# Grouped-query attention over a cached K and V: units of four kv heads of two sequences, K turned by VectorE in 32x32 blocks instead of by TensorE

## The chip, the cores and the metric

One core of one Trainium2 chip runs the whole program. The metric is the time of one execution of the program on the device in microseconds (us); the median of several executions counts. TensorE (PE) multiplies matrices, VectorE (DVE) and ScalarE (ACT) work on elements, GpSimd (POOL) does small copies, SyncE (SP) issues the transfers from the memory of the device (HBM) to the memory of the core, which has 128 partitions.

## The reference

Eight sequences bring 4 new tokens each. Queries are projected from x, scored against a cached K of 2048 keys, and the softmax weighs a cached V. 32 query heads share 8 kv heads, four to one. All inputs are bf16.

```python
# B, Sq, D = 8, 4, 512;  Hq, Hkv, Sk, Dh = 32, 8, 2048, 128
q = (x @ wq).reshape(B, Sq, Hq, Dh).transpose(0, 2, 1, 3)
k = jnp.repeat(k_cache, 4, axis=1)          # k_cache, v_cache: [8, 8, 2048, 128]
v = jnp.repeat(v_cache, 4, axis=1)
scores = jnp.einsum("bhqd,bhkd->bhqk", q, k) * (Dh ** -0.5)
p = softmax(scores, axis=-1)
o = jnp.einsum("bhqk,bhkd->bhqd", p, v)
return o.transpose(0, 2, 1, 3).reshape(B, Sq, Hq * Dh) @ wo   # [8, 4, 512]
```

K and V are 33.6 MB each, wq and wo 4.2 MB each: 75.5 MB are read once.

## The kernel before

A unit is two kv heads of one sequence; there are 32 units. Its K is one transfer of 1 MiB (`load_k`, L113): partition g*64+s holds 32 consecutive keys of head g, a row of 8 KiB in HBM. V is loaded in the same way (`load_v`, L123). K has 7 buffers and V has 6. All loads are issued by SP in one written order. At most eight transfers are under way at once, because each issue waits for the completion of the transfer eight before it.

Scores need K with the head dimension on the partitions. `transpose_part` (L193) does a quarter of a unit: PE turns four 128x128 tiles, each element a pair of bf16 taken as one 32-bit word, into PSUM (L198), and VectorE copies the quarter to the core's memory (L200). `scores` (L254) multiplies it with block-diagonal queries, four products beside each other in four 32-column groups of the array (L261), and ScalarE takes the exponential and its sum (L272). `probs_to_keys` (L277) turns the probabilities on PE and ScalarE copies them into a block-diagonal tile (L286). `values` (L316) holds a 128x128 piece of V as weights and streams 32 columns of probabilities through it, 32 times a unit. `norms` and `finish` divide by the sums. `to_tokens`, `to_wo_rows` and `project` bring the result to the rows in which wo is loaded and multiply with wo. Half of wo is loaded late, into the place of wq.

The order of each engine's work is the order in which the program is written (`manual_schedule`). The main loop (L405) runs iteration n with K of unit n turned, scores of n-1 and values of n-2. Each engine takes its instructions in this order, and waits on semaphores for the others.

Of the kernel before, what the change touches and what calls it, by code (L numbers as in the profile page):

```python
# [8 lines left out]
BF16 = mybir.dt.bfloat16  # L9
FP32 = mybir.dt.float32  # L10
EXP = mybir.ActivationFunctionType.Exp


@with_exitstack
def kernel(
# [18 lines left out]
    G2 = Hkv // 2  # L34
    C = 2 * Sk // 128
    NQ = 2 * rep * Sq
    HQ = rep * Sq
    J = C // 2
    JT = J // 4
    HP = 2 * rep  # L40
    scale = float(Dh) ** -0.5
    NU = G2 * B
    KB = 7
    VB = 6
    A = 2
    KA = A + 1
    WR = HP
    DH = D // 2


    NE, WE, WM, WN = 40, 8, 5, 64
    assert NE * WE + 128 * WM + WN == HP * 128
    AX = mybir.AxisListType.X
    ADD = mybir.AluOpType.add
    assert Dh == 128 and C == 32 and NQ == 32 and G2 == 4

    const = ctx.enter_context(tc.tile_pool(name="const", bufs=1))
    wpool = ctx.enter_context(tc.tile_pool(name="wpool", bufs=1))
    kpool = ctx.enter_context(tc.tile_pool(name="kpool", bufs=KB))
    vpool = ctx.enter_context(tc.tile_pool(name="vpool", bufs=VB))  # L60
    ktpool = ctx.enter_context(tc.tile_pool(name="ktpool", bufs=6))
    small = ctx.enter_context(tc.tile_pool(name="small", bufs=2))
    psum_k = ctx.enter_context(tc.tile_pool(name="psum_k", bufs=3, space=bass.MemoryType.PSUM))
    psum_s = ctx.enter_context(tc.tile_pool(name="psum_s", bufs=1, space=bass.MemoryType.PSUM))
    psum_t = ctx.enter_context(tc.tile_pool(name="psum_t", bufs=1, space=bass.MemoryType.PSUM))
    psum_o = ctx.enter_context(tc.tile_pool(name="psum_o", bufs=1, space=bass.MemoryType.PSUM))
    psum_e = ctx.enter_context(tc.tile_pool(name="psum_e", bufs=1, space=bass.MemoryType.PSUM))
    psum_l = ctx.enter_context(tc.tile_pool(name="psum_l", bufs=1, space=bass.MemoryType.PSUM))


    order = ctx.enter_context(tc.manual_schedule())


    pad0 = const.tile([128, 192], BF16, name="pad0")
    wo_e = const.tile([64, WE, D], BF16, name="wo_e")
    wo_n = const.tile([WN, D], BF16, name="wo_n")
    wo_m = const.tile([128, WM, D], BF16, name="wo_m")
    x_sb = const.tile([T, D], BF16, name="x_sb")
    wq_sb = wpool.tile([128, R, HqDh], BF16, tag="w", name="wq_sb")
    xT_sb = const.tile([128, R, T], BF16, name="xT_sb")  # L80
    qT_all = const.tile([128, G2, B, HP, Sq], BF16, name="qT_all")


    q_bd = const.tile([128, G2, 2, B, 2, 2, HQ], BF16, name="q_bd")
    pick = const.tile([128, 2, 2, Dh // 2], BF16, name="pick")
    ident4 = const.tile([128, 128], FP32, name="ident4")

    groups = [(0,), (1, 2), (3,)]
    oT = [const.tile([128, HP, len(ps), B, Sq], BF16, name=f"oT{ps[0]}") for ps in groups]
    out_sb = const.tile([2 * T, DH], BF16, name="out_sb")  # L90
    oP12 = const.tile([128, WR, 2, T], BF16, name="oP12")
    nat_sb = const.tile([2 * T, HP * 128 + 24 * WE], BF16, name="nat_sb")
    oP3 = const.tile([128, WR, T], BF16, name="oP3")
    oP = [None, oP12[:, :, 0, :], oP12[:, :, 1, :], oP3[:, :, :]]
    oE = const.tile([64, WE, T], BF16, name="oE")
    oM = const.tile([128, WM, T], BF16, name="oM")
    oN = const.tile([WN, T], BF16, name="oN")
    ident = const.tile([128, 128], BF16, name="ident")
    by_q = const.tile([128, HQ], FP32, name="by_q")
    ones = const.tile([128, 128], FP32, name="ones")  # L100
    pad = const.tile([128, 96], BF16, name="pad")
    probs = [const.tile([128, C, 2, HQ], BF16, name=f"probs{i}") for i in range(3)]

    units = [(p, b) for p in range(G2) for b in range(B)]
    ks = [None] * NU
    vs = [None] * NU

    def load_k(u):
        if u >= NU:
            return  # L110
        p, b = units[u]
        ks[u] = kpool.tile([128, C, Dh], BF16, tag="k_sb", name="k_sb")
        nc.sync.dma_start(  # L113
            ks[u][:, :, :],
            k_cache[b, 2 * p : 2 * p + 2].rearrange("g (s c) d -> (g s) c d", c=C),
        )

    def load_v(u):
        if u >= NU:
            return  # L120
        p, b = units[u]
        vs[u] = vpool.tile([128, C, Dh], BF16, tag="v_sb", name="v_sb")
        nc.sync.dma_start(  # L123
            vs[u][:, :, :],
            v_cache[b, 2 * p : 2 * p + 2].rearrange("g (s c) d -> (g s) c d", c=C),
        )

    def load_wo_e(i):

        hi, m = divmod(i, 4)  # L130
        rows = wo[: NE * WE, :].rearrange("(q r) j -> q r j", r=WE)
        a, b = hi * 32 + m, hi * NE // 2 + m
        nc.sync.dma_start(wo_e[a : a + 17 : 4, :, :], rows[b : b + 17 : 4, :, :])

    def load_wo_m():
        nc.sync.dma_start(wo_n[:, :], wo[HP * 128 - WN : HP * 128, :])
        nc.sync.dma_start(
            wo_m[:, :, :], wo[NE * WE : HP * 128 - WN, :].rearrange("(q r) j -> q r j", r=WM)
        )

    def load_wo(p, r0, n):
        rows = wo[p * HP * 128 : (p + 1) * HP * 128, :].rearrange("(q r) j -> q r j", r=WR)
        nc.sync.dma_start(wo_sb[:, p - 1, r0 : r0 + n, :], rows[:, r0 : r0 + n, :])

    load_k(0)
    nc.sync.dma_start(wq_sb[:, :, :], wq.rearrange("(p r) n -> p r n", r=R))
    nc.sync.dma_start(x_sb[:, :], x.flatten_outer_dims())
    loads = []
    for u in range(NU + KA):
        if 1 <= u <= 8:  # L150
            loads.append(("e", u - 1))
        if 0 < u < NU:
            loads.append(("k", u))
        if u == NU + 2:
            loads.append(("m", 0))
        if u >= KA - 1 and u - KA + 1 < NU:
            loads.append(("v", u - KA + 1))
    loads.reverse()

    def load_ready(nk, nv):  # L160

        while loads:
            kind, u = loads[-1]
            if kind in "em":
                loads.pop()
                load_wo_e(u) if kind == "e" else load_wo_m()
                continue
            if u >= (nk + KB if kind == "k" else nv + VB):
                return
            loads.pop()  # L170
            (load_k if kind == "k" else load_v)(u)

    nc.gpsimd.memset(wo_e[:, :, :], 0.0)
    load_ready(0, 0)

    make_identity(nc, ident[:])
    make_identity(nc, ident4[:])
    for e in range(2):
        for g in range(2):
            nc.vector.tensor_copy(  # L180
                out=pick[:, e, g, :], in_=ident[:, :].rearrange("d (k e) -> d e k", e=2)[:, e, :]
            )
    nc.vector.memset(q_bd[:, :, :, :, :, :, :], 0.0)
    for t in probs:
        nc.vector.memset(t[:, :, :, :], 0.0)
    nc.vector.memset(ones[:, :], 1.0)
    nc.vector.tensor_reduce(
        out=by_q[:, :], in_=ident4[:, :].rearrange("p (c q) -> p q c", q=HQ), axis=AX, op=ADD
    )
# [296 lines left out]
```

## Time and profile before

| What | Value |
|---|---|
| median of three runs | 190.75 us (190.39 to 193.14) |
| span of the profiled execution, first to last instruction | 187.5 us (its own whole time is not listed) |
| median less span | 3.25 us |
| busy: PE, VectorE, ScalarE, GpSimd | 143.8, 108.6, 69.5, 4.6 us |
| bytes moved, mean rate | 75.92 MB, 405 GB/s |
| rate of DMA from 20 to 165 us | 424 to 425 GB/s |
| mean granted clock of TensorE | 0.954 |

Busy time is time in which an engine executes; the span also has its waits. A matmul that is pipelined with others has a duration longer than the step from one to the next, so PE's costs are read from steps where there are rows of them. A group's row gives the line, the engine, the operation, output and inputs, the shapes, the count, the busy time, the mean duration, and the idle time before with what ended it.

### The profile page before, as it was taken

Reading aid. Unit: us, or ns where it says so; the run is one execution under the profiler, and the core shown is the slowest. Engines: PE = TensorE matmul, PEld = TensorE weight load, DVE = VectorE, ACT = ScalarE, POOL = GpSimd, SP = SyncE. Lnnn points to the kernel's source line nnn. Section 1 sums busy time; section 2 is a strip of 40 time slices with the busy share of each in tenths; the row PEclk is TensorE's granted clock in tenths of the full one; section 3 lists DMA queues with packets and bytes.
Section 4 is the critical chain, followed back from the end, with each engine's and each line's share of the span. In section 5 each row is a group of like instructions: output and inputs, shape, how many; then the busy total and the mean of one; then the engine's idle time right before and its main releaser. Section 6 shows DMA issues by size and latency. Waiting matters only on the chain.

```text
span 187.5 us, 5636 instructions
## 1 busy us (share of the span) xinstructions
PE 143.8 (77%) x2474; PEld 119.1 (63%) x2474; DVE 108.6 (58%) x217; ACT 69.5 (37%) x202; POOL 4.6 (2%) x9
## 2 busy tenths in 40 slices
PE   0516799977879988898788888787787888878493
PEld 0506488866658867786676766566676677667272
DVE  0850698757527766577565657575565666663120
ACT  2001664553324444153344444433344443425200
POOL 8100000000000000000000000000000000000000
PEclk9975999999969999999999999999999999999759
DMA  5999999999999999999999999999999999999970
GB/s 204 467 447 379 421 435 416 425 426 425 425 425 428 421 423 423 430 421 428 425 428 421 428 425 418 428 428 418 430 426 419 425 426 428 419 426 408 409 277 12
DMA packets 10984, 75.92 MB, mean 405 GB/s; under 512 B 1288, under 2 KB 1448, under 8 KB 2600
## 3 DMA queue, kind: packets, MB, share of 16 engines
q1 hardware_dynamic: 10912, 75.55, 96.2%
q8 instruction: 19, 0.31, 0.6%
q14 instruction: 5, 0.04, 0.1%
q10 hardware_dynamic: 48, 0.02, 0.0%
HBM read 75.53 MB, written 0.03 MB: 403 GB/s over the span
## 4 chain that ended last, share of the span: by engine, by line
DMA 92%; PE 6%; SPq 0%; issue 0%; ACT 0%; DVE 0%
DMA k_sb<-in_k_cache_dram 58%; DMA v_sb<-in_v_cache_dram 18%; DMA wo_m<-in_wo_dram 9%; DMA wq_sb<-in_wq_dram 8%; PE out_ps L397 3%; PE kp L198 1%; PE o_ps L321 1%; PE nat L345 0%; SPq L113 0%; PE perm L367 0%; PE s_ps L261 0%; ACT out_sb L453 0%; DVE oT L332 0%
## 5 line engine op out<-in xcount | busy, mean ns | idle before, releaser
L200 DVE COPY kt<-kp 128x1024 bf16<-128x1024 bf16 x128 | 82.3, 685 | 38.6 <-PE kp L198 38.4
L198 PE MATMUL kp<-ident,k_sb 128*128 128x128 f32 x512 | 71.3, 284 | 24.3 <-DMA k_sb<-in_k_cache_dram 22.7
L198 PEld LDWEIGHTS kp<-ident,k_sb 128*128 128x128 f32 x512 | 57.0, 144 | 36.0 <-issue 18.5
L286 ACT COPY probs<-pt 64x512 bf16<-64x512 bf16 x64 | 37.1, 580 | 53.1 <-PE pt L280 52.7
L272 ACT ACTIVATE s_sb<-s_ps 128x256 bf16<-128x256 f32 x64 | 24.0, 380 | 34.1 <-PE s_ps L261 21.7
L321 PE MATMUL o_ps<-probs,v_sb 128*128 128x32 bf16 x1024 | 30.7, 177 | 2.0 <-DMA v_sb<-in_v_cache_dram 1.2
L321 PEld LDWEIGHTS <-v_sb 128*128 128x128 bf16 x1024 | 29.8, 96 | 3.7 <-DMA v_sb<-in_v_cache_dram 2.8
L261 PE MATMUL s_ps<-kt,q_bd 128*32 128x256 bf16 x512 | 20.9, 282 | 0.0
L261 PEld LDWEIGHTS <-q_bd 128*32 128x32 bf16 x512 | 10.6, 95 | 6.2 <-issue 5.4
L311 DVE RECIPROCAL r_sb<-l_ps 128x64 f32<-128x64 f32 x16 | 8.9, 557 | 8.6 <-PE l_ps L303 8.6
L272 ACT ACTIVATION_READ_ACCUMULATOR s_sb<-s_ps 128x1 f32 x64 | 12.7, 198 | 0.0
L280 PE MATMUL pt<-ident,s_sb 128*128 128x128 bf16 x128 | 12.3, 218 | 0.0
L303 PE MATMUL l_ps<-by_gq,ones 128*128 128x64 f32 x32 | 6.9, 297 | 5.2 <-DVE by_gq L296 5.2
L332 DVE TENSOR_TENSOR oT<-o_ps,r_sb 128x32 bf16<-128x32 f32 x32 | 6.1, 191 | 6.5 <-PE o_ps L321 5.9
L303 PEld LDWEIGHTS l_ps<-by_gq,ones 128*128 128x128 f32 x32 | 4.8, 188 | 6.7 <-DVE by_gq L296 4.9
L280 PEld LDWEIGHTS <-s_sb 128*128 128x128 bf16 x128 | 8.8, 104 | 0.2 <-ACT s_sb L272 0.2
L227 ACT ACTIVATE qT_all<-psq 128x256 bf16<-128x256 f32 x4 | 1.5, 385 | 16.6 <-PE psq L220 16.6
L245 DVE CAST q_bd<-pse 64x512 bf16<-64x512 f32 x4 | 2.6, 682 | 4.3 <-PE pse L236 4.3
L296 DVE TENSOR_TENSOR by_gq<-l_sb,by_q 128x64 f32<-128x64 f32 x16 | 3.5, 216 | 2.1 <-ACT s_sb L272 2.1
L397 PE MATMUL out_ps<-wo_sb,oP 128*32 128x256 bf16 x48 | 4.4, 336 | 0.0
L210 PE MATMUL xtp<-ident,x_sb 32*128 32x32 bf16 x4 | 0.3, 192 | 4.8 <-DMA x_sb<-in_x_dram 4.8
L453 ACT CAST out_sb<-out_ps 64x256 bf16<-64x256 f32 x1 | 0.4, 366 | 9.6 <-PE out_ps L397 9.6
(45 smaller groups left out, 43.0 us busy)
## 6 DMA issues: line engine op xcount, KB each, us to landing
k_sb<-in_k_cache_dram SPq DMA_DIRECT2D x32, 1024.0 KB, 19.6
v_sb<-in_v_cache_dram SPq DMA_DIRECT2D x32, 1024.0 KB, 13.3
wq_sb<-in_wq_dram SPq DMA_DIRECT2D x1, 4096.0 KB
wo_sb<-in_wo_dram SPq DMA_DIRECT2D x4, 512.0 KB
wo_sb<-in_wo_dram SPq DMA_DIRECT2D x4, 256.0 KB, 8.1
wo_m<-in_wo_dram SPq DMA_DIRECT2D x1, 640.0 KB
wo_e<-in_wo_dram SPq DMA_DIRECT2D x8, 40.0 KB
wo_n<-in_wo_dram SPq DMA_DIRECT2D x1, 64.0 KB, 18.2
```

The costliest lines, as they stand in the source:

```text
L198: nc.tensor.transpose(kp[:, j, :], k4[:, w : w + 128], ident4[:, :])
L200: nc.vector.tensor_copy(out=k_t[:, :, :, :].rearrange("k j s e -> k (j s e)"), in_=kp[:, :, :].rearrange("k j s -> k (j s)").bitcast(BF16),)
L261: nc.tensor.matmul(s_ps[t * 32 : (t + 1) * 32, :, g, :], lhsT=q_bd[:, p, e, b, g, :, :], rhs=kt[(u, t)][:, :, g * 64 : (g + 1) * 64, e], s ...
L272: nc.scalar.activation(out=s_sb[:, :, g, :], in_=s_ps[:, :, g, :], func=EXP, accum_out=l_sbs[u][:, u % 2, g : g + 1])
L280: nc.tensor.transpose(pt[:, j, :], s_sbs[u][:, j, :, :].rearrange("q g s -> q (g s)"), ident[:, :])
L286: nc.scalar.copy(out=pr[rows, :, g, :], in_=pt[rows, :, :].rearrange("s j (c q) -> s (j c) q", q=HQ),)
L296: nc.vector.tensor_tensor(out=by_gq[:, :, :, :], in0=l_sbs[u][:, :, :].unsqueeze(3).to_broadcast([128, 2, 2, HQ]), in1=by_q[:, :].unsqueez ...
L303: nc.tensor.matmul(l_ps[:, :, :].rearrange("d u q -> d (u q)"), lhsT=ones[:, :], rhs=by_gq[:, :, :, :].rearrange("k u g q -> k (u g q)"), ...
L311: nc.vector.reciprocal(r_sb[:, :, :], l_ps[:, :, :])
L321: nc.tensor.matmul(o_ps[:, :], lhsT=vs[u][:, 2 * (t * JT + j) + c, :], rhs=pr[:, i, :, :].rearrange("s g q -> s (g q)"), start=(i == 0), s ...
L332: nc.vector.tensor_tensor(out=oT[(p + 1) // 2][:, :, (p == 2) * 1, b, :], in0=o_pss[u][:, :].rearrange("d (h s) -> d h s", h=HP), in1=r_sb ...
L397: nc.tensor.matmul(out_ps[half * T : (half + 1) * T, :], lhsT=o, rhs=w[:, half * DH : (half + 1) * DH], start=(p == 0 and r == 0), stop=(p ...
```

## The change

A unit becomes four kv heads of two sequences; there are 8 units. K and V of one sequence of a unit come as one transfer of 2 MiB, 16 KiB a partition: partition g*32+s holds 64 consecutive keys of head g. The transfers go to a ring of eight such places, `ring`, which also receives wq (two places) and wo (two places). A load may be written once the place eight loads before it is given back. All loads are still issued by SP and with at most eight under way.

K is turned by VectorE alone, in 32x32 blocks of 32-bit words (`turn`), from the ring to six buffers of 128x1024 words. A block leaves one head's 32 words of a key on 32 partitions, so a score needs two products for the two halves of the words and two for the two halves of a pair; the queries are block-diagonal over the four heads (`queries`, small copies on GpSimd, for the next unit), and all 128 rows and columns of the array are used. The scores of a unit fill four banks of PSUM (`s_ps`, one tile, one buffer): 128 queries by 2048 keys. VectorE then takes the maximum of each query, in two halves (`top`), ScalarE the exponential with that maximum as its bias (`exps`). VectorE turns the probabilities in blocks, and ScalarE copies them, 32 partitions at a time, into block-diagonal weights (`weights`). `values` now loads the probabilities as weights and streams V of both sequences, 256 columns, through them, 64 times a unit. `scaled` divides on ScalarE, `by_heads` sorts the rows by a product with a permutation, `to_rows` turns them to the rows of wo. All products with wo stand at the end.

The first wait of `top` in an iteration stands on its first reduction; the second has none of its own. On ScalarE `scaled(u - 1)` stands behind the eight copies of `weights(u)`; on PE `by_heads(6)` stands ahead of `values(7)`.

```diff
-    units = [(p, b) for p in range(G2) for b in range(B)]
+    units = [(gg, bp) for gg in range(NG) for bp in range(NP)]
+    loads = [("k", 0, 0), ("x",), ("wq", 0), ("wq", 1), ("k", 0, 1), ("k", 1, 0), ("k", 1, 1)]
+    for u in range(NU):
+        if u + 2 < NU:
+            loads += [("v", u, 0), ("v", u, 1), ("k", u + 2, 0), ("k", u + 2, 1)]
+    loads += [("v", NU - 2, 0), ("v", NU - 2, 1), ("vlast", NU - 1), ("wo", 0), ("wo", 1)]
...
-    def transpose_part(u, t):
-        kp = psum_k.tile([128, JT, 128], FP32, tag="k", name="kp")
...
+    def turn(u, b, t):
+
+        kt = ktpool.tile([128, CT, J, S, 2], BF16, tag="kt", name="kt")
+        n = CT * Dh
+        nc.vector.transpose(
+            out=kt[:, :, :, :, :].rearrange("w c j s e -> w (c j s e)").bitcast(FP32),
+            in_=ring[:, slot_of["k", u, b], t * n : (t + 1) * n].bitcast(FP32),
+        )
+        kts[u, b, t] = kt
...
+    s_ps = psum_s.tile([128, NT, 512], FP32, name="s_ps")
+
+    def scores(u, t):
+        for b in range(NB):
+            for j in range(J):
+                for e in range(2):
+                    nc.tensor.matmul(
+                        s_ps[:, t, :],
+                        lhsT=q_bd[u % 2][:, b, 2 * j + e, :, :, :].rearrange("w g b q -> w (g b q)"),
+                        rhs=kts[u, b, t][:, :, j, :, e],
+                        start=(b == 0 and j == 0 and e == 0),
+                        stop=(b == NB - 1 and j == J - 1 and e == 1),
+                    )
...
+    def top(u, h):
...
+        nc.vector.tensor_reduce(
+            out=stats[u][0][:, h : h + 1],
+            in_=s_ps[:, 2 * h : 2 * h + 2, :].rearrange("q t n -> q (t n)"),
+            axis=AX,
+            op=ALU.max,
+            negate=True,
+        )
+        if h == 1:
+            nc.vector.tensor_scalar(
...
+    def exps(u, h):
...
+        nc.scalar.activation(
+            out=p_sb[:, :, :, :].rearrange("q c s e -> q c e s"),
+            in_=s_ps[:, 2 * h : 2 * h + 2, :].rearrange("q t (c e s) -> q (t c) e s", e=2, s=S),
+            func=EXP,
+            bias=stats[u][1][:, :],
+            scale=scale,
+            accum_out=stats[u][2][:, h : h + 1],
+        )
...
+    def weights(u, h):
+        pt = small.tile([128, CH // 2, 32, 2], BF16, tag="pt", name="pt")
+        nc.vector.transpose(
+            out=pt[:, :, :, :].rearrange("s c q e -> s (c q e)").bitcast(FP32),
+            in_=ps[u, h][:, :, :, :].rearrange("q c s e -> q (c s e)").bitcast(FP32),
+        )
+        pb = pbs[u, h] = p_bd[(2 * u + h) % 4]
+        for g in range(G):
+            rows = slice(g * 32, (g + 1) * 32)
+            nc.scalar.copy(out=pb[rows, :, g, :, :], in_=pt[rows, :, :, :])
...
+    def values(u, h):
...
+        for i in range(CH):
+            nc.tensor.matmul(
+                o_pss[u][:, :, :],
+                lhsT=pbs[u, h][:, i // 2, :, :, i % 2].rearrange("s g q -> s (g q)"),
+                rhs=v[:, :, h * CH + i, :],
+                start=(h == 0 and i == 0),
+                stop=(h == 1 and i == CH - 1),
+            )
...
+    for u in range(NU + 1):
+        if u < NU:
+            for t in range(NT):
+                turn(u, 1, t)
+            for t in range(NT):
+                scores(u, t)
+                if t == 0 and u >= 2:
+                    by_heads(u - 2)
+            if u >= 2:
+                to_rows(u - 2)
+            if u + 1 < NU:
+                queries(u + 1)
+            for h in range(2):
+                top(u, h)
+            for h in range(2):
+                exps(u, h)
+            for h in range(2):
+                weights(u, h)
+            norm(u)
+        else:
+            by_heads(u - 2)
+            to_rows(u - 2)
+        if u >= 1:
+            values(u - 1, 0)
+            values(u - 1, 1)
+            scaled(u - 1)
+        if u + 1 < NU:
+            for t in range(NT):
+                turn(u + 1, 0, t)
+        issue(5 + 4 * u)
+    by_heads(NU - 1)
+    to_rows(NU - 1)
+    for gg in range(NG):
+        for g in range(G):
+            project(gg, g, 0, 4)
```

## The prediction

> **What bounds the kernel now.** I read the page's parts 1 to 4 first: busy time, the 40 slices, the chain that ended last. Then rows of single operations, then granted clock by stretches.
>
> ```profile
> PEclk9975999999969999999999999999999999999759
> DMA  5999999999999999999999999999999999999970
> GB/s 204 467 447 379 421 435 416 425 426 425 425 425 428 421 423 423 430 421 428 425 428 421 428 425 418 428 428 418 430 426 419 425 426 428 419 426 408 409 277 12
> DMA 92%; PE 6%; SPq 0%; issue 0%; ACT 0%; DVE 0%
> ```
>
> The transfers are the bound. They run in every slice but the first and the last two, at about 425 GB/s, and 92% of the chain is DMA. PE (143.8 us) and VectorE (108.6) have slack. What follows the last transfers is short: PE's last product ends at 184.5 us, the span at 187.5.
>
> So two questions decide: what the longer rows do to the rate, and whether the new work of each engine still hides under the transfers, in the loop and behind the last K.
>
> **Longer rows.** In 173 to 178 us rows of 5 and 4 KiB move at 401 GB/s; rows of 8 KiB at 425. On one of 16 DMA engines that is 163 ns for 4 KiB (taking all as 4) and 308 ns for 8 KiB, 145 ns for 4 KiB more. So 16 KiB takes 308 + 290 = 598 ns: 438 GB/s. Bounds: no gain (425), or 438; I take 435. K and V (67.1 MB) would need 154.3 us in place of 157.9. That counts only if DMA stays the bound.
>
> **The prices of the new loop.**
>
> ```profile
> L200 DVE COPY kt<-kp 128x1024 bf16<-128x1024 bf16 x128 | 82.3, 685 | 38.6 <-PE kp L198 38.4
> L272 ACT ACTIVATE s_sb<-s_ps 128x256 bf16<-128x256 f32 x64 | 24.0, 380 | 34.1 <-PE s_ps L261 21.7 <-issue 9.0 <-ACT probs L286 3.4
> L286 ACT COPY probs<-pt 64x512 bf16<-64x512 bf16 x64 | 37.1, 580 | 53.1 <-PE pt L280 52.7
> L321 PE MATMUL o_ps<-probs,v_sb 128*128 128x32 bf16 x1024 | 30.7, 177 | 2.0 <-DMA v_sb<-in_v_cache_dram 1.2 <-ACT probs L286 0.7
> L245 DVE CAST q_bd<-pse 64x512 bf16<-64x512 f32 x4 | 2.6, 682 | 4.3 <-PE pse L236 4.3
> L236 PE MATMUL pse<-qT_all,pick 128*128 128x512 bf16 x4 | 1.5, 376 | 1.3 <-ACT q_bd L245 1.0 <-ACT qT_all L227 0.2
> ```
>
> *PE.* 32 columns take 177 ns and 512 take 376 (L321, L236), so a column in a stream costs 0.415 ns: 0.212 us for 512 columns, 0.106 for 256. *ScalarE.* 256 elements take 380 ns, 512 take 580: 0.78 ns each and 0.18 us fixed, so 0.98 for 1024. Before has no ScalarE copy from the core's memory; I use the same line. *VectorE.* Copies of 256 and 512 bf16 (L369: 291 and 425 ns) give a fixed 0.157 us; L245 leaves 1.025 ns for a 32-bit element. A reduction of 1024 is 1.2 us, a turn of 512 words 0.68.
>
> **The unknown: x, one turn of 1024 words.** Before shows none. From below, L200 moves 1024 items in 0.685. From above, every word is taken twice (fill a block, then empty it): 2.26. I take one word at a time by L245, 1.21, the nearest row in width. [...]
>
> **One iteration, on VectorE's queue.** It runs `turn(u,1)`, `top`, `weights`, `norm`, `turn(u+1,0)` in that order, so VectorE stands while PE scores and ScalarE exponentiates. From the start of `turn(u,1)`:
> - The first turn ends at 1.21; 28 of 32 score products and `by_heads` are still to come: 0.1 (handoff, by the gap from L261 to L272) + 28 x 0.212 + 0.1 + 0.27 (end of the last, handoff) = 7.6. The other three turns and `to_rows` (0.5) lie beside this.
> - `top` is behind the last score in both halves: 2 x 1.2 makes 10.0, the small scaling 10.3.
> - Two exponentials, 2 x 0.98 + 0.2 of handoffs: 12.45. The second turn of probabilities 0.1 + 0.68, `norm` 0.35: 13.6.
> - `turn(u+1,0)`, 4 x 1.21: 18.4 us.
>
> Behind these waits on VectorE's queue stand the next unit's turns, and PE waits for them. `values(u-1)` (64 x 0.106 = 6.8) and the four score products already possible end at about 15.5; PE then has nothing until 19.7, about 4 us of idleness an iteration.
>
> **The clock** makes that idleness cost.
>
> ```profile
> 51.00:52.00 1.00, 0.33 (x8) 1.00 1.01 426
> 52.00:53.00 1.00, 0.04 (x1) 1.00 1.06 451
> 53.00:54.00 1.00, 1.00 (x6) 0.57 0.97 410
> 54.00:55.00 1.00, 1.00 (x12) 0.50 1.01 426
> 55.00:56.00 1.00, 1.00 (x18) 0.50 0.99 418
> 56.00:57.00 1.00, 1.00 (x9) 0.72 1.11 459
> ```
>
> The columns are the stretch, its length, PE busy (count), clock, DMA share, GB/s. An idle time of 1.62 us is followed by about 3 us at half clock, though PE is busy again. The same comes after an idle 174 to 176.2, then until 182.4. So I charge 3 us at half clock to each iteration's scores: 1.5 us lost, 19.9 us an iteration.
>
> **Against the transfers.** wq landed at 15.3 us (the chain: issued at 1.19, 14.14 long) after 5.24 MB: 3.0 us and 425 GB/s. In the new order K(0,1) is behind 8.42 MB: 22.8 us, the start of iteration 0. K(7,1) is behind 62.95 MB: 151.1 at 425, 147.7 at 435. VectorE gets there at 22.8 + 7 x 19.9 = 162.1. It would keep up only with 17.8 to 18.3 us an iteration. The loop is thus bound by VectorE's queue, not DMA; a place of the ring comes back in time (K(u,0) when iteration u begins, needed some 17 us later), so transfers don't stop but end early, and the rate of the rows is worth nothing.
>
> **The tail, from the start of iteration 7.** Scores 7.6 + 1.5 = 9.1; `top` and scaling 11.8; exponentials 13.95. ScalarE's eight copies of 0.98: 21.8, with `scaled(6)` behind them 22.3. `by_heads(6)` waits for that and holds up `values(7)` on PE: 22.75. PE has idled some 6 us, so values take 6.8 + 1.5 + 0.17: 31.2. `scaled` 31.7, `by_heads` 32.15, `to_rows` 32.9. 64 products with wo at 0.076 (the 40 at the end took 3.04): 37.8. ScalarE 38.3, out transfer and end 2.6 (184.9 to 187.5): 40.9. Before did most of its products with wo under the transfers.
>
> **The sum.** 162.1 + 40.9 = 203.0, against the span of 187.5: +15.5. The median stands 3.25 above the span: 206 us, 8% slower. About 2% is what a measurement can tell from no change. Costed at nothing: GpSimd's copies of queries (a whole iteration to hide in; without it some 2 us), loading weights (an L321 load and product take 0.03 us a pair, hidden by 0.106), and two waits for the ring.
>
> **Rivals.**
> - *The clock stays full.* Then 18.4 an iteration: 22.8 + 128.8 = 151.6, just with K(7,1); the tail 37.9: 189.5, so 193 us, +1%. This is the case that isn't slower: from 18.3 us an iteration down DMA sets the pace again and only the tail differs. A turn at L200's 0.685 ends there too (17.3 an iteration with the half clock; 151.1 + 40.4, so 194 to 195 at 425 GB/s, 191 at 435). For it: 14 of 18.4 us of PE are busy. Against: 1.62 us sufficed at 53 us. [...] 18%.
> - *A turn takes each word twice,* 2.26: scores end with the turns at 11.2, the iteration takes 25.5, start of the last 201, tail 43.5: 248 us. 14%.
> - *DMA stays the bound and longer rows pay:* 3.6 us less, and 1.5 less behind the last piece of wo: 182.4, 186 us. It needs no more than 29.5 us (six places) behind K(7,1); ScalarE's copies, values and `top` alone make 17, and the handoffs in order the rest. 4%.
> - *The rows don't raise the rate:* changes nothing in the forecast.
>
> **How the numbers follow.** Forecast 62% (198 to 222: x from 1.1 to 1.4, 1 to 6 us at half clock), then 18, 14 and 4%; 2% for what I don't see. The range holds forecast and first rival: 190 to 223; left out are the double turn and the faster case, 20%. Faster 0.04; same 0.18; slower 0.78.
>
> **What would show it.** Of the profile after: turns near 1.2 us; VectorE's `top` waiting for PE and its turns of probabilities for ScalarE in each iteration; PEclk near 0.8 to 0.9 with dips in the loop; DMA slices falling before the end; `by_heads` waiting for ScalarE near 180 us. Iterations of 18 us or less, or a tail under 33, would prove me wrong.

## The result

The changed kernel takes 209.76 us (median of 4 runs, 206.65 to 213.04) against 191.94 us (190.39 to 194.37) of the kernel before: 1.096 times as long, 95% interval 1.083 to 1.109. The forecast was 206 us, slower with a chance of 0.78. The profiled execution took 208.7 us; its span is 206.9, so 1.8 us lie around the span, where I had put 3.25. Below, spans are compared with spans: 187.5 us before, 206.9 after, 203.0 forecast. One thing is needed to read some numbers further down: in five of the profiled executions below the transfers ran at about 360 to 400 GB/s in place of 430 over the first 60 to 80 us, and the spans of those kernels' other executions stand beside them.

### The profile after

Slices of the changed kernel (clock, DMA share, GB/s), and the first line of the chain that ended last:

```profile
PEclk9999999658997999799979996999699969996799
DMA  6999999999999999999999999999999999600000
GB/s 206 434 431 431 431 434 431 437 424 434 424 437 424 435 424 437 421 440 423 437 424 437 424 435 424 431 428 434 428 437 412 429 418 422 245 0 0 0 3 6
issue 5%; PE 2%; ACT 2%
```

Before, DMA ran to the end and made 92% of the chain. Now the transfers end in slice 35, about 178 us, and for 26 us nothing moves: they have lost the lead. The rows of 16 KiB run at 430 GB/s (429 to 432 from 10 to 150 us) against 424 to 425 of the rows of 8 KiB; that gain buys nothing, since nobody waits for it. PEclk shows a dip in nearly every iteration. The chain's line covers only the last 9% of the span, so the loop is read from the timeline.

The costliest groups (line, engine, operation, output and input, shapes, count | busy us, mean ns | idle before, and what ended it):

```profile
L189 PE MATMUL s_ps<-kt,q_bd 128*128 128x512 bf16 x256 | 71.8, 435 | 37.4 <-DVE kt L166 36.1
L166 DVE STREAM_TRANSPOSE kt<-ring 128x1024 f32<-128x1024 f32 x64 | 73.0, 1208 | 2.1 <-DMA ring<-in_k_cache_dram 2.1
L244 ACT COPY p_bd<-pt 32x1024 bf16<-32x1024 bf16 x64 | 66.6, 1040 | 0.7
L223 ACT ACTIVATE p_sb<-s_ps,stat 128x1024 bf16<-128x1024 f32 x16 | 22.0, 1404 | 75.9 <-DVE stat L210 75.9
L202 DVE TENSOR_REDUCE stat<-s_ps 128x1 f32<-128x1024 f32 x16 | 18.8, 1219 | 35.6 <-PE s_ps L189 35.6
L237 DVE STREAM_TRANSPOSE pt<-p_sb 128x512 f32<-128x512 f32 x16 | 11.4, 712 | 18.1 <-ACT p_sb L223 18.1
```

Every engine waits for the next one in a ring: PE for VectorE's turns (36.1 us), VectorE for PE's scores (35.6) and for ScalarE's exponentials (18.1), ScalarE for the maximum (75.9). No engine is busy for more than 67% of the span. VectorE waits for a transfer only 2.1 us, up to the loop's first turn at 23.2 us.

### One iteration

Timeline of the changed kernel (start, duration, what, count, [idle before <- releaser]); first VectorE, then PE, then ScalarE:

```profile
79.26 9.11 DVE L166 STREAM_TRANSPOSE kt<-ring 128x1024 f32<-128x1024 f32 x8
93.42 2.36 DVE L202 TENSOR_REDUCE stat<-s_ps 128x1 f32<-128x1024 f32 x2 [4.53 <-PE s_ps L189]
97.63 0.71 DVE L237 STREAM_TRANSPOSE pt<-p_sb 128x512 f32<-128x512 f32 x1 [1.60 <-ACT p_sb L223]
98.97 0.71 DVE L237 STREAM_TRANSPOSE pt<-p_sb 128x512 f32<-128x512 f32 x1 [0.63 <-ACT p_sb L223]
99.84 4.61 DVE L166 STREAM_TRANSPOSE kt<-ring 128x1024 f32<-128x1024 f32 x4
```

```profile
80.64 1.03 PE L189 MATMUL s_ps<-kt,q_bd 128*128 128x512 bf16 x4 [0.84 <-DVE kt L166]
85.05 1.75 PE L189 MATMUL s_ps<-kt,q_bd 128*128 128x512 bf16 x4 [3.38 <-DVE kt L166]
87.21 0.37 PE L282 MATMUL o_pm<-o_sb,perm 128*128 128x128 bf16 x2 [0.41 <-ACT o_sb L273]
87.38 6.01 PE L189 MATMUL s_ps<-kt,q_bd 128*128 128x512 bf16 x24
93.23 7.15 PE L261 MATMUL o_ps<-ring,p_bd 128*128 128x256 bf16 x64
```

```profile
78.26 8.40 ACT L244 COPY p_bd<-pt 32x1024 bf16<-32x1024 bf16 x8
86.68 0.47 ACT L273 ACTIVATE o_sb<-o_ps,stat 128x256 bf16<-128x256 f32 x1
```

The eight turns at 79.26 are four of `turn(3,0)` and, from about 83.8, four of `turn(3,1)`. VectorE then stands 4.53 us for the scores and 1.60 + 0.63 for the exponentials. The next group of turns starts at 99.84: a period of 20.58 us. PE stands 3.38 us for the first of `turn(3,1)`. After four products it waits again, 0.41 us, for ScalarE: `by_heads(1)` needs `scaled(1)`, which stands behind the eight copies of L244.

From the start of `turn(3,1)`, step by step:

| Step | forecast, us | measured, us |
|---|---|---|
| turn, scores to the last product | 9.1 | 9.6 (83.8 to 93.4) |
| two reductions and the scaling | 2.7 | 2.7 (to 96.15, start of the exponential) |
| two exponentials | 2.15 | 2.8 (to 98.9) |
| turn of the probabilities, `norm` | 1.15 | 0.9 (to 99.84) |
| four turns of the next unit | 4.84 | 4.56 |
| one iteration | 19.9 | 20.6 |

### The tail

Timeline of PE at the end of the changed kernel:

```profile
175.27 7.15 PE L261 MATMUL o_ps<-ring,p_bd 128*128 128x256 bf16 x64
189.83 0.37 PE L282 MATMUL o_pm<-o_sb,perm 128*128 128x128 bf16 x2 [7.41 <-ACT o_sb L273]
190.00 9.32 PE L261 MATMUL o_ps<-ring,p_bd 128*128 128x256 bf16 x64
200.13 3.67 PE L301 MATMUL out_ps<-ring,oP 128*32 128x256 bf16 x64
```

`by_heads(6)` waits 7.41 us for `scaled(6)`, behind ScalarE's eight copies, and holds up `values(7)`, as forecast. The last iteration starts at 166.0 (162.1 forecast), and from there to the end it takes 40.9 us, exactly the forecast; two errors within it cancel (below).

### The profile page after: what moved, and what is told of

Read it like the earlier page. It is cut to its first block, busy times and chain, and to the rows that moved or that the text cites. A ratio compares the mean times of both kernels' runs of the same rounds, so it can differ in the third digit from the quotient of the medians.

```text
span 206.9 us, 2262 instructions
## 1 busy us (share of the span) xinstructions
PE 139.2 (67%) x884; PEld 83.7 (40%) x884; DVE 116.7 (56%) x147; ACT 94.9 (46%) x109; POOL 19.9 (10%) x76
## 5 line engine op out<-in xcount | busy, mean ns | idle before, releaser
L189 PE MATMUL s_ps<-kt,q_bd 128*128 128x512 bf16 x256 | 71.8, 435 | 37.4 <-DVE kt L166 36.1
L166 DVE STREAM_TRANSPOSE kt<-ring 128x1024 f32<-128x1024 f32 x64 | 73.0, 1208 | 2.1 <-DMA ring<-in_k_cache_dram 2.1
L244 ACT COPY p_bd<-pt 32x1024 bf16<-32x1024 bf16 x64 | 66.6, 1040 | 0.7
L261 PE MATMUL o_ps<-ring,p_bd 128*128 128x256 bf16 x512 | 59.3, 278 | 0.0
L189 PEld LDWEIGHTS <-q_bd 128*128 128x128 bf16 x256 | 26.4, 106 | 77.1 <-issue 53.3
L223 ACT ACTIVATE p_sb<-s_ps,stat 128x1024 bf16<-128x1024 f32 x16 | 22.0, 1404 | 75.9 <-DVE stat L210 75.9
L261 PEld LDWEIGHTS <-p_bd 128*128 128x128 bf16 x512 | 51.1, 100 | 8.5
L202 DVE TENSOR_REDUCE stat<-s_ps 128x1 f32<-128x1024 f32 x16 | 18.8, 1219 | 35.6 <-PE s_ps L189 35.6
L178 POOL COPY q_bd<-qT 32x64 bf16<-32x64 bf16 x64 | 13.3, 229 | 115.8 <-PE s_ps L189 82.7
L237 DVE STREAM_TRANSPOSE pt<-p_sb 128x512 f32<-128x512 f32 x16 | 11.4, 712 | 18.1 <-ACT p_sb L223 18.1
## 6 DMA issues: line engine op xcount, KB each, us to landing
ring<-in_v_cache_dram SPq DMA_DIRECT2D x14, 2048.0 KB, 20.5
ring<-in_v_cache_dram SPq DMA_DIRECT2D x4, 1024.0 KB, 19.8
```

The costliest lines, as they stand in the source:

```text
L166: nc.vector.transpose(out=kt[:, :, :, :, :].rearrange("w c j s e -> w (c j s e)").bitcast(FP32), in_=ring[:, slot_of["k", u, b], t * n : ( ...
L178: nc.gpsimd.tensor_copy(out=qb[rows, b, :, g, b, :].rearrange("w (j e) q -> w j e q", e=2), in_=qT[rows, gg, :, NB * bp + b, :, :, :].rear ...
L189: nc.tensor.matmul(s_ps[:, t, :], lhsT=q_bd[u % 2][:, b, 2 * j + e, :, :, :].rearrange("w g b q -> w (g b q)"), rhs=kts[u, b, t][:, :, j, ...
L202: nc.vector.tensor_reduce(out=stats[u][0][:, h : h + 1], in_=s_ps[:, 2 * h : 2 * h + 2, :].rearrange("q t n -> q (t n)"), axis=AX, op=ALU.max,
L223: nc.scalar.activation(out=p_sb[:, :, :, :].rearrange("q c s e -> q c e s"), in_=s_ps[:, 2 * h : 2 * h + 2, :].rearrange("q t (c e s) -> q ...
L237: nc.vector.transpose(out=pt[:, :, :, :].rearrange("s c q e -> s (c q e)").bitcast(FP32), in_=ps[u, h][:, :, :, :].rearrange("q c s e -> q ...
```

## The experiments

The theory (A in the expectations): **the period is a ring of waits** (a circle of engines that wait for each other, not the buffer `ring`) through VectorE's order (turns, maximum, turns of the probabilities, next turns), PE's order and ScalarE's order, lengthened by stretches at half clock that PE's idle time brings. The rivals: the half clock as the whole loss (B in those of e2 and e3), the transfers, a single slow operation, or the mere amount of work on VectorE (C). The experiments are named as in the expectations (e2, e3, ...). An iteration is read from one profiled execution of each kernel.

### e2: no maximum

```diff
-            for h in range(2):
-                top(u, h)          # two reductions and the scaling
+            top(u)                 # only makes the tiles of the sums
...
-            bias=stats[u][1][:, :],
```

> The reductions to the maximum and the scaling of it are left out; the exponential is taken of the scaled scores directly, as the kernel before does. Theory A: 2.75 us go from each iteration's chain (2.36 of reductions, 0.4 of scaling and handoff), 17.8 us an iteration, just the pace of the transfers; the tail is 2.75 shorter too: span 186 to 190. Theory B: the scores still start at half clock; only the reductions' own time can go, so no less than A says and rather more: 190 to 200. If the reductions were hidden beside other work: 205 to 207.

The kernel before takes no maximum either, so this is also work that the change added. Measured: span 193.8 us, 1.032 times the kernel before (1.024 to 1.040). Early in the run the period is 17.8 us (turns at 38.26 and 56.03). The same iteration of the changed kernel took 20.17 (38.44 to 58.61), so 2.4 us came off it: the 2.36 of the reductions, not quite the 2.75 expected. From 74.85 us on VectorE waits for K instead. Page of e2, GB/s and two groups:

```profile
GB/s 200 413 396 392 389 386 379 382 386 399 389 389 379 386 386 399 404 433 430 431 426 433 431 426 430 430 433 433 433 433 433 426 433 433 409 424 416 420 173 7
L166 DVE STREAM_TRANSPOSE kt<-ring 128x1024 f32<-128x1024 f32 x64 | 73.7, 1211 | 17.4 <-DMA ring<-in_k_cache_dram 16.9
L206 ACT ACTIVATE p_sb<-s_ps 128x1024 bf16<-128x1024 f32 x16 | 20.4, 1300 | 63.6 <-PE s_ps L189 63.6
```

The transfers are the bound again (16.9 us of waiting for K), and in this execution they ran at 379 to 413 GB/s for 75 us. At 388 in place of 430 GB/s that costs some 7 us by an estimate from these rows, about the distance from the 186 to 190 that theory A expected; no execution of e2 shows the shorter span (the others have 194.0 to 200.4). The 193.8 lies in the range of theory B too, so e2 does not tell the two apart; e3 and e35 do. That the ring had held back the transfers, and not the reverse, stands. Without the bias the exponential takes 1.30 us in place of 1.40.

### e3: unread products keep TensorE busy

```diff
         for b in range(NB):
+            if b == 1 and t == 0 and u >= 1:
+                keep_busy(u, 14)
```

`keep_busy` issues 14 products of 512 columns into a sum that nobody reads, in `scores`, while PE would wait for the first turn of the second sequence.

> 14 products of 512 columns, whose result nobody reads, fill TensorE's idle time between the first four and the next four score products of each iteration from 1 on (about 3.0 of 3.4 us). Theory A with its term for the clock: the scores run at full clock, 1.5 to 2 us less an iteration, 18.6 to 19.1 us, last iteration starts at 153 to 156, tail up to 1.5 less in its scores: span 192 to 197, granted clock above 0.97 in the loop. If the half clock is not what lengthens the scores, or VectorE has slack there: 204 to 208. If the half clock were all of the loss (B): 188 to 190.

Measured: span 203.5, ratio 1.076 (1.067 to 1.086): 3.4 us less than the changed kernel, where 10 to 15 were expected. The changed kernel's own executions have spans of 204.9 to 211.3, so the gain is read from the iteration. Timeline of PE in e3:

```profile
84.26 1.03 PE L202 MATMUL s_ps<-kt,q_bd 128*128 128x512 bf16 x4 [0.36 <-DVE kt L166]
86.43 0.27 PE L295 MATMUL o_pm<-o_sb,perm 128*128 128x128 bf16 x2 [1.14 <-ACT o_sb L286]
86.54 5.39 PE L202 MATMUL s_ps<-kt,q_bd 128*128 128x512 bf16 x24
```

From iteration 1 on the loop has no half-clock stretch any more: four products take 1.03 us in place of 1.75, 24 take 5.39 in place of 6.01, together 1.34 us less. But PE comes to `by_heads` sooner and now waits 1.14 us for ScalarE in place of 0.41. The period falls only to 19.9 to 20.2. The next wait was close behind the clock: `scaled(u-2)` behind eight copies, which I had costed in the tail and not in the loop.

### e5: the scaling between the two halves of the copies

```diff
-            for h in range(2):
-                weights(u, h)
+            weights(u, 0)
+            if u == 0:
+                weights(u, 1)
...
             scaled(u - 1)
+            if u < NU:
+                weights(u, 1)
```

> On ScalarE the scaling of the unit before stands between the two halves of the copies of probabilities instead of behind both; on VectorE the second turn of probabilities stands behind the norm. Theory A: in the tail the sorting product no longer holds up the last values until all eight copies are done; values start near 186 instead of 190 and their second half is bound by the last copies: 5 to 6 us less; in the loop the sorting product no longer waits 0.4 us ahead of most scores: 0 to 3 us less. Span 198 to 202. If the last values wait for V or for the copies anyway: 205 to 207.

Measured: span 201.1, ratio 1.065 (1.058 to 1.073), as expected. In the loop `by_heads` no longer waits, yet the period falls only by 0.2, to 20.36 (mean of four from 78.89 to 160.31): PE gets to the 24 products earlier, and more of them fall into the half clock (they begin at 86.0 in place of 87.4, ahead of the same end of it, and take 6.69 us in place of 6.01). In the tail `by_heads(6)` waits 3.19 us in place of 7.41, and the tail is 36.2 in place of 40.9. So the order on ScalarE costs 4.7 us in the tail.

### e35: both

> The 14 unread products an iteration and the earlier scaling on ScalarE together. With the unread products alone an iteration took 19.95 us instead of 20.58, since the sorting product then stood 1.1 us waiting for the scaling ahead of 24 score products. Theory A, with the clock term worth 1.5 us once that wait is gone: 18.7 to 19.0 us an iteration, last iteration starts at 155 to 157, tail 36 as with the earlier scaling alone: span 191 to 194. If the clock is worth no more than the 0.6 us seen alone: span 196 to 200.

Measured: span 193.7, ratio 1.024 (1.008 to 1.040), as expected. Timeline of VectorE in e35, where the starts of the groups of eight turns give the period:

```profile
80.06 9.09 DVE L166 STREAM_TRANSPOSE kt<-ring 128x1024 f32<-128x1024 f32 x8
98.65 9.09 DVE L166 STREAM_TRANSPOSE kt<-ring 128x1024 f32<-128x1024 f32 x8
117.57 9.09 DVE L166 STREAM_TRANSPOSE kt<-ring 128x1024 f32<-128x1024 f32 x8
136.18 9.09 DVE L166 STREAM_TRANSPOSE kt<-ring 128x1024 f32<-128x1024 f32 x8
154.79 9.09 DVE L166 STREAM_TRANSPOSE kt<-ring 128x1024 f32<-128x1024 f32 x8
```

18.6 to 18.9 us, 18.68 on average. Each edit alone brought 0.2 and 0.6 us an iteration, both together 1.9: while one of the two waits stands, it takes up most of what the other gives. Once ScalarE's order is out of the way, the half clock is worth 1.7 us an iteration (20.36 to 18.68); the prediction charged 1.5. In this execution the transfers ran at 379 to 401 GB/s up to about 70 us, and the loop started at 25.1 us in place of 23.1; without that the span would be some 2 us shorter.

### e4: exponentials that write contiguously

```diff
-            out=p_sb[:, :, :, :].rearrange("q c s e -> q c e s"),
-            in_=s_ps[:, 2 * h : 2 * h + 2, :].rearrange("q t (c e s) -> q (t c) e s", e=2, s=S),
+            out=p_sb[:, :, :, :],
+            in_=s_ps[:, 2 * h : 2 * h + 2, :].rearrange("q t (c e s) -> q (t c) s e", e=2, s=S),
```

The changed kernel reads the sums in order and writes every other bf16; this one takes the sums in pairs that lie 32 apart and writes in order.

> The exponential of 1024 took 1.40 us where 0.98 was predicted from shorter rows. Here it reads PSUM in the order of the output and writes without gaps, where it wrote every second bf16; the results are the same. If the gapped write is the cause: 1.05 to 1.1 us each, 0.65 us less an iteration, span 200 to 203 (changed kernel: 205 to 207). If reading in steps of 32 words costs as much: 1.4 us, span 205 to 207. If the per-partition bias is the cause (1.30 without it): 1.4 us as well.

Measured: span 211.2, ratio 1.126 (1.104 to 1.149). The interval overlaps that of the changed kernel (1.083 to 1.109), so the runs show no gain rather than a sure loss. The operation behaved as expected and the kernel did not. Two groups of e4:

```profile
L189 PE MATMUL s_ps<-kt,q_bd 128*128 128x512 bf16 x256 | 79.6, 471 | 34.0 <-DVE kt L166 32.7
L223 ACT ACTIVATE p_sb<-s_ps,stat 128x1024 bf16<-128x1024 f32 x16 | 17.7, 1109 | 84.9 <-DVE stat L210 84.9
```

The exponential is 0.295 us shorter (1.109 in place of 1.404), so the write with gaps is most of what made it longer than forecast. The products became longer, 471 ns in place of 435. The granted clock shows why. Busy time by stretches (stretch, length, busy us and count of PE, PEld, DVE, ACT and POOL, granted clock, DMA share, GB/s), of the changed kernel and of e4, each cut at the times at which the clock changes:

```profile
81.80:85.22 3.42, 0.17 (x1) 0.10 (x1) 3.42 (x4) 3.38 (x4) 0.00 (x0) 1.00 1.04 446
85.22:88.63 3.41, 3.00 (x9) 1.05 (x8) 3.38 (x5) 1.90 (x3) 0.00 (x0) 0.50 0.98 418
88.63:92.04 3.41, 3.41 (x17) 1.52 (x16) 0.26 (x1) 0.00 (x0) 0.00 (x0) 1.00 1.03 442
```

```profile
102.09:105.50 3.41, 1.23 (x6) 0.41 (x5) 3.41 (x4) 3.37 (x4) 0.00 (x0) 1.00 0.99 418
105.50:108.92 3.42, 1.86 (x4) 0.54 (x4) 3.42 (x4) 3.37 (x4) 0.00 (x0) 0.50 0.99 426
108.92:112.33 3.41, 3.13 (x9) 1.19 (x9) 1.93 (x4) 0.23 (x1) 0.00 (x0) 0.50 1.02 437
```

In the records the clock changes only on a grid of 3.413 us. In both kernels PE idles 3.38 us ahead of `turn(u,1)`. In the changed kernel that idle time fills one interval of the grid, and one interval at half clock follows. In e4 it lies across a boundary of the grid, at 105.5: the interval that holds its first part has PE busy for 1.23 us and is followed by half clock; the next holds the rest, only 1.86 us of work at half clock, and is followed by half clock again. In total 58.0 us at half clock in place of 37.5. The period is 21.7 us on average (five from 57.75 to 166.08) in place of 20.5: 0.6 us gained on ScalarE, and some 1.7 lost on PE. What differs in the two traces is the phase of the idle time against the grid. All four executions of e4 have a lower mean clock (0.847 to 0.864) than those of the changed kernel (0.871 to 0.909).

### e345: e35 with the contiguous exponentials

Were the clock the whole reason for e4's loss, the same edit must pay where TensorE is kept busy.

> The edits of e35 (14 unread products in each iteration, the scaling between the two halves of the copies) and of e4 (exponentials that write contiguously) together. Theory A (a contiguous exponential is 0.295 us shorter on the path, and e4 lost that only because its iterations fell into two half-clock windows): two exponentials in each of eight iterations, 8 x 0.59 = 4.7 us off the 193.7 of e35, so a span of 188 to 190.5, the exponential at about 1.11 us, and few half-clock stretches inside the loop. Theory B (the contiguous form itself costs something elsewhere on the path): 194 or more, with the granted clock as in e35.

Measured: the profiled execution took 189.14 us, span 187.4, a little below the range of theory A. Three other executions have spans of 191.4 to 196.7, and what their transfers did was not recorded, so the span decides nothing and the iteration has to. The half clock is 13.7 us in all, as in e35, and none of it lies between 45 and 170 us. Slices of e345:

```profile
PEclk9999999657999999999999999999999999997899
```

The period falls from 18.68 to 18.19, by 0.49 where 0.59 was expected; a further 2.0 us of the 6.3 between the two spans comes from the loop's start (23.08 us against 25.09: K(0,1) landed earlier), and does not belong to the edit. By the iteration theory A holds.

### v2: without the maximum, and with what the runs above taught

```diff
-    s_ps = psum_s.tile([128, NT, 512], FP32, name="s_ps")
+    s_pss = [psum_s.tile([128, 2, 512], FP32, name=f"s_ps{h}") for h in range(2)]
...
-                if t == 0 and u >= 2:
-                    by_heads(u - 2)
...
-                to_rows(u - 2)
+                by_heads(u - 2)
...
-            for h in range(2):
-                top(u, h)
+            top(u)
...
+            if u >= 2:
+                to_rows(u - 2)
...
-    by_heads(NU - 1)
-    to_rows(NU - 1)
+    for u in range(NU - 2, NU):
+        by_heads(u)
+        to_rows(u)
```

with the contiguous exponentials of e4 besides.

> The maximum left out as in the kernel before, exponentials written without gaps from two separate halves of the scores so that the first can start after half of them, the sorting product behind all scores, and in the last pass behind the last values. Theory A: 16 to 17.5 us an iteration, so transfers set the pace: K(7,1) lands near 149.5 at 430 GB/s; values of the last unit end 24 to 26 us later and are ahead of the last piece of wo, which lands near 179.5; then four products, the copy and the output: span 182 to 185, below the kernel before (187 to 189). If transfers run at 388 GB/s in the first 75 us as they did without the maximum: 189 to 192. If something else holds the loop: above 192.

Measured: span 183.9, ratio 0.975 (0.959 to 0.992), as expected. Page of v2:

```profile
GB/s 196 435 428 431 435 424 435 435 435 424 428 431 431 426 438 420 435 428 428 428 435 438 420 435 431 424 428 442 438 420 435 420 435 420 420 428 419 422 364 21
DMA 60%; PE 31%; DVE 3%; issue 2%; SPq 2%; ACT 1%; ACTq 0%
L166 DVE STREAM_TRANSPOSE kt<-ring 128x1024 f32<-128x1024 f32 x64 | 73.8, 1212 | 19.8 <-DMA ring<-in_k_cache_dram 19.8
```

The transfers run to the end at about 430 GB/s, DMA is the largest part of the chain again (60%), VectorE waits 19.8 us for K. Stretches of 3.4 us at half clock still occur, four behind iteration 0, and the kernel keeps the pace of the transfers all the same. Like the kernel before, this one leaves out the maximum, so the next three ask whether the bound can be reached with the maximum.

### v3: e345 with the score sums in two tiles

```diff
-    s_ps = psum_s.tile([128, NT, 512], FP32, name="s_ps")
+    s_pss = [psum_s.tile([128, 2, 512], FP32, name=f"s_ps{h}") for h in range(2)]
...
-            in_=s_ps[:, 2 * h : 2 * h + 2, :].rearrange("q t n -> q (t n)"),
+            in_=s_pss[h][:, :, :].rearrange("q t n -> q (t n)"),
```

> e345 with the score sums in two tiles, so that the first reduction need not wait for the products of the second half. Theory A (the two reductions stood one after the other behind the last product only because they read one tile): one reduction of 1.2 us leaves the path in each iteration, 8 to 9.6 us off the 188 to 190.5 of e345, down to the floor that the transfers set, 184 in v2; so 182 to 186, and VectorE waiting for K. Theory B (VectorE's order, or the unread products, hold the first reduction back): 187 to 191.

Measured: three executions with spans of 183.9 to 184.2 (185.75, 186.00, 185.73 us), ratio 0.973 (0.967 to 0.980): within the range of theory A, at the floor of v2. The profiled execution has 191.3. Its rows, with the same row of e345 in the second fence:

```profile
GB/s 202 414 373 384 384 377 370 377 366 384 380 373 380 384 385 435 435 435 438 411 432 432 428 432 432 438 425 428 428 425 435 435 425 438 413 425 425 415 393 36
L215 DVE TENSOR_REDUCE stat<-s_ps 128x1 f32<-128x1024 f32 x16 | 19.3, 1209 | 15.7 <-PE s_ps L202 15.7
```

```profile
L215 DVE TENSOR_REDUCE stat<-s_ps 128x1 f32<-128x1024 f32 x16 | 18.8, 1219 | 23.6 <-PE s_ps L202 23.6
```

VectorE's wait for the scores falls from 23.6 to 15.7 us, 1.0 an iteration: in the changed kernel the first reduction waited for products of the second half that it doesn't read, since both lay in one tile.

### e56: two turns in the gap

```diff
             for h in range(2):
                 exps(u, h)
+            if u + 1 < NU:
+                for t in range(2):
+                    turn(u + 1, 0, t)
...
         if u + 1 < NU:
-            for t in range(NT):
+            for t in range(2, NT):
                 turn(u + 1, 0, t)
```

on e5.

> e5 with two of the next unit's four turns of K moved into the gap in which VectorE waits for the exponentials (2.2 us of idle in each iteration of the changed kernel); no work is added or taken away, and no buffer is added. Theory A (the order of the turns on VectorE, behind the chain of one unit's softmax, sets the period): the iteration falls from 20.3 by about 2.2 us to 18.1 or less, since TensorE then waits 1.2 and not 3.4 us for its next turn, and the last iteration starts at about 150; behind it the tail of e5, 36.2: a span of 186 to 191. Theory C (the amount of work on VectorE sets the time, not its place): 198 to 202, as e5. Should K land later than the two turns are due, VectorE waits for it ahead of the turn of the probabilities, and the span is 191 to 196.

Timeline of VectorE in e56:

```profile
37.79 2.36 DVE L166 STREAM_TRANSPOSE kt<-ring 128x1024 f32<-128x1024 f32 x2
41.64 6.86 DVE L166 STREAM_TRANSPOSE kt<-ring 128x1024 f32<-128x1024 f32 x6
55.35 2.37 DVE L166 STREAM_TRANSPOSE kt<-ring 128x1024 f32<-128x1024 f32 x2
75.99 2.37 DVE L166 STREAM_TRANSPOSE kt<-ring 128x1024 f32<-128x1024 f32 x2 [4.26 <-DMA ring<-in_k_cache_dram]
```

The same iteration in e5:

```profile
38.42 9.11 DVE L166 STREAM_TRANSPOSE kt<-ring 128x1024 f32<-128x1024 f32 x8
58.61 9.09 DVE L166 STREAM_TRANSPOSE kt<-ring 128x1024 f32<-128x1024 f32 x8
```

The period that no transfer holds back, 37.79 to 55.35, is 17.56 us; in e5 (38.42 to 58.61) it is 20.19. The work is the same and only its place differs, so theory C (the amount of work) falls. From 75.99 on VectorE waits for K (15.8 us over the whole run): in this execution the transfers ran at 362 to 408 GB/s for the first 65 us, and the span is 197.4, just above the expectation's third case (191 to 196). Of the three others one has a span of 187.8, in theory A's range, and two have 195.6 and 199.5. The spans alone therefore do not decide; the iteration does.

### v4: all of it, with the whole computation

e56 with the contiguous exponentials and the two tiles of sums.

> The whole computation with the maximum: e56 with contiguous exponentials and the score sums in two tiles, without unread products. Theory A: 0.59 and 1.2 us more come off each iteration of e56, which brings it below the period of the transfers (four transfers of 2 MiB at 430 GB/s, 19.5 us, less the lead that the eight places give), so it is paced by them like v2: 182 to 187, VectorE waiting for K. The other case: TensorE idles while it waits for K, and half-clock windows come of it: 188 to 195.

Measured: three executions with spans of 185.0 to 185.2, ratio 0.979 (0.970 to 0.987); the profiled one took 192.2, with transfers at 382 to 402 GB/s for its first 60 us and 19.3 us of VectorE waiting for K, and a fifth 191.9. The three lie in theory A's range, the two in that of the other case. The kernel keeps the change's layouts and the whole computation, has no unread products, and in those three executions is faster than the kernel before by about 2%.

### e1b: the next unit's turns ahead of the maximum

```diff
-    ktpool = ctx.enter_context(tc.tile_pool(name="ktpool", bufs=6))
+    ktpool = ctx.enter_context(tc.tile_pool(name="ktpool", bufs=8))
...
-    p_bd = [const.tile([128, CH // 2, G, 32, 2], BF16, name=f"p_bd{i}") for i in range(4)]
+    p_bd = [const.tile([128, CH // 2, G, 32, 2], BF16, name=f"p_bd{i}") for i in range(3)]
```

with the four turns of the next unit moved ahead of the reductions. With all four buffers of weights the same order does not fit (e1): eight buffers of turned K leave 2.97 kB a partition, and the pool `small` needs 9.75.

> The order of the first experiment again, with room for it: eight buffers of turned K, and three in place of four buffers of block-diagonal probabilities (no wait comes of that by the trace: the buffer is read 6 us before it is written). The four turns of the next unit's first K stand ahead of the maximum. Theory A (order on VectorE's queue): beside the scores these 4.6 us cost nothing, about 16.2 us an iteration; so VectorE soon waits for K(u+1,0) instead, which lands 4.9 us ahead of K(u+1,1), and now holds up the maximum behind it: the last iteration starts 11.1 us (4.6 of turns, 6.5 of maximum, exponential and turns of probabilities) after that K, landing near 144.5, so at 155 to 156 in place of 166; tail 41 as before: span 194 to 199. Theory C (amount of VectorE's work, the same 117 us): 204 to 208.

Measured: span 274.3, ratio 1.463 (1.437 to 1.488). It tells nothing about the order of the turns, by a fault of the experiment: with three buffers of weights, those of unit u's second half are written into the buffer that `values(u-1, 0)` reads, and stand ahead of it in the program. PE then waits for ScalarE's copies in each iteration. Waits in e1b (engine, line, releaser: us in all, times, longest):

```profile
PE o_ps L261 <- ACT p_bd L244: 103.2, 7, 19.3
```

Its statement that no wait comes of three buffers was wrong, and by the order of the program its values come from the newer probabilities. e56 put the same question without taking a buffer away.

## Why the prediction was right

- **The bound.** The loop passes from DMA to VectorE's queue, and the transfers end early: right (zeros in the last slices). e2, v2, v3 and v4 show the other side: shorten the ring enough and the transfers set the time again, at 184 to 185 us. The rows of 16 KiB gave 430 GB/s, between the bounds of 425 and 438; the value of 435 was too high, and made no difference.
- **The unknown, one turn of 1024 words.** Forecast 1.21 by a row of the same width, measured 1.208, and 1.13 from one to the next. The rival of a double turn (248 us) is refuted. A turn of 1024 words takes the time that a reduction of 1024 takes (1.22).
- **The iteration.** 19.9 forecast, 20.58 measured in this one, 20.4 on average from 23.2 to 166.0. The mis-sized term is the exponential: 0.98, drawn from reads and writes without gaps, where the change writes every other bf16 and takes 1.40. e4 shows that the gaps make 0.295 of it; the rest is a contiguous 1.11 against 0.98, of which the bias is 0.09 (v2, contiguous and without it: 1.02). Two of them are 0.65 us more with their handoffs. The other miss is a wait: `by_heads(u-2)` stands for ScalarE in every iteration, 0.41 us, where I had it only in the tail. The turns of K and of the probabilities were 0.5 us shorter than charged. Net 0.5 us on average, seven times, and 0.4 at the start (23.2 against 22.8), make 3.9 us: the last iteration starts at 166.0 and not at 162.1, which is the whole miss of the span (206.9 against 203.0).
- **The clock.** 3 us at half clock an iteration, 1.5 us lost: measured 3.41 and, by e35 against e5, 1.7. PE's idle time was 3.38 and not about 4. That it cost one interval and not two, as in e4, goes in the two traces with the phase of the idle time, which the prediction did not consider; so far the term is luck. The rival in which the clock stays full (193 us, a span of 189.5) falls by the trace: one interval at half clock in each iteration from 64.7 us on. e35 shows what the full clock would be worth. That PE is busy most of the time, which spoke for that rival (14 of 18.4 us; measured 76.7 of the 100 us from 50 to 150), did not keep the clock full: in the changed kernel the idle 3.38 us fill one interval nearly whole (0.17 us of work from 81.80 to 85.22) and half clock follows, and in e4 half clock follows an interval with PE busy for 1.23 of 3.41 us.
- **The tail.** 40.9 forecast and measured, partly by luck: ScalarE's copies took 8.4 in place of 7.85, the exponentials 2.8 in place of 2.15, and `values(7)` 9.3 in place of 8.45, while the 64 products with wo took 3.67 in place of 4.9 (the row that priced them, 181.43 to 184.47, ran at half clock up to 182.85) and began without waiting for `to_rows`. e5 shows the mechanism: with the scaling ahead of four of the copies the tail falls to 36.2.
- **The time around the span.** 1.8 us here, against 3.25, taken from a median and a span of different executions. That error takes 1.45 us off the 3.9 by which the span was missed, which leaves 2.45 against the profiled 208.7; the median of 209.76 lies 1 us higher.

## What to carry to other kernels

Where several engines hand one unit's work around in a ring, write down the period as the longest way round, wait by wait, and look on every engine's queue for what stands behind the waiting instruction: here three waits of 0.4 to 2.6 us an iteration (the first reduction behind products that it does not read, the scaling behind eight copies, the turns behind the exponentials) and a write pattern made the difference between 207 and 185 us, with nothing left out. Two waits in parallel hide each other, so one mended alone shows little (0.2 and 0.6 us, together 1.9). A price drawn from a row of the same operation did not hold for another access pattern: the exponential took 1.40 us with the gaps in its write and 1.11 without (e4).

## What the runs showed of the hardware

- **The clock's grid.** In the records of thirteen profiles of this case, the two kernels' and the experiments', TensorE's granted clock is 1.00 or 0.50 and changes only on a grid of 3.413 us. The intervals at full clock from about 20 us on, by PE's busy time in them and the clock of the next interval: with less than 1.3 us of work in 3.41, the next was at half clock in 53 of 53; from 1.3 to 1.55 us in 11 of 17; with more in none of over 450. So in these traces an interval in which PE worked for less than 38% was always followed by half clock, and one in which it worked for more than 45% never. The 1.62 us of idleness in the kernel before, quoted in the prediction, fit: the interval that held them, 49.73 to 53.14, has 1.38 us of work, and half clock follows.
- **The phase counts.** Since 20.5 us is six intervals (6 x 3.413) and the period is 20.4 to 20.8 from 58.61 us on, the idle time of the changed kernel falls at nearly the same place of the grid in each iteration, and one interval is at half clock; in e4 there are two each time. A change of 0.6 us in the two exponentials shifted the total at half clock from 37.5 to 58.0 us. The four executions of the changed kernel have mean clocks of 0.908, 0.909, 0.894 and 0.871 and spans of 204.9, 206.9, 209.1 and 211.3; whether the phase is why is not shown.
- **Slower transfers at the start.** e2, e35, e56, v3 and v4 were profiled with 362 to 404 GB/s from the third slice through the first 60 to 80 us, then 430; in the changed kernel, e345 and v2, with the same list of transfers, there were 430 throughout. v3's profiled execution has a span of 191.3 and its others 184; that the transfers make this difference is not shown, since those of the others were not recorded. The cause of the slower stretch is open.
